# Window attention on one core: the square of a copied score tile as a 16-bit step of VectorE, 288 tiles off ScalarE, and a new order

## The chip, the cores and the metric

The kernel runs on one core of a Trainium2 chip. The metric is the device time of one execution in microseconds (us). The core has five engines that run side by side, each through its own instruction list in order, and that wait for each other by semaphores: TensorE (PE, matrix products into PSUM), ScalarE (ACT, here the exponential), VectorE (DVE), GpSimd (POOL, which works from SBUF to SBUF) and SyncE (SP, which issues DMAs).

## The reference

An image x of 224 x 224 pixels with 96 channels is projected to q, k and v. The first 48 channels attend within horizontal stripes 8 rows high, the last 48 within vertical stripes 8 columns wide, and the two halves are put side by side and projected once more.

```python
qkv = jnp.einsum('bhwc,cd->bhwd', x, wqkv)
q, k, v = qkv[..., :C], qkv[..., C:2 * C], qkv[..., 2 * C:]
scale = C2 ** (-0.5)                                   # C = 96, C2 = 48, sw = 8
qh = q[..., :C2].reshape(B * nh, sw * W, C2)           # 28 stripes of 1792 tokens
ah = _softmax(jnp.einsum('bqc,bkc->bqk', qh, kh) * scale, axis=-1)
oh = jnp.einsum('bqk,bkc->bqc', ah, vh).reshape(B, H, W, C2)
...                                                    # ov: the same over vertical stripes, channels C2:
o = jnp.pad(oh, ((0, 0), (0, 0), (0, 0), (0, C2))) + jnp.pad(ov, ((0, 0), (0, 0), (0, 0), (C2, 0)))
return jnp.einsum('bhwc,cd->bhwd', o, wo)
```

There are 56 stripes. Each needs 1792 x 1792 scores, and an exponential of every score.

## The kernel before

The stripes are done in 28 pairs P, one stripe in each half of the partitions. The 1792 queries of a pair are cut into chunks c of 512, 512, 512 and 256, and its keys into 14 groups of 128. A *tile* is a chunk against one group of keys (two groups for the short chunk): 128 partitions by 1024 scores, in two banks of PSUM. There are 28 x 49 = 1372 tiles, and there are three ways from scores to weights.

- *On ScalarE.* TensorE forms the scores (L670), ScalarE takes the exponential of all 1024 columns into a buffer PT in SBUF (L888), and TensorE multiplies it with V (L696). There were 1090 such tiles.
- *Off ScalarE, uncopied.* The scores are formed in banks 6 and 7 (L683). The exponential is made by writing the bits of a 16-bit float: the low part of the fixed-point score is the fraction, whose polynomial is a square plus a constant. VectorE takes the low half of each 32-bit score out of PSUM into a buffer `qb` (L1189), and the banks are given back. GpSimd squares it into PT (L1105). TensorE forms the same scores a second time, and VectorE adds their high part to the square (L1199). There were 180.
- *Off ScalarE, copied.* VectorE copies the whole 32-bit scores to `qb` (L1188), and TensorE need not form them again. Four steps follow: a shift and scale of the low halves into PT (L1108), the square in place in PT (L1109), a scale back into the low halves of `qb` (L1110), and the last conversion of `qb` to the bits in PT (L1111). Before, all four were GpSimd's. There were 102.

There are sixteen PT buffers, six `qb` buffers and three `tmp` buffers. VectorE also takes K, Q and V from PSUM to SBUF (L440, L451, L488) and the products with V (L1164), and it normalises the projected output: for the horizontal stripes into `Ph_sb` (L537, L545), for the vertical ones with `Ph_sb` added. That last step is done either in single tiles on VectorE (L593), or as a product of up to five tiles on VectorE into `tmp` (L580) with the sum on GpSimd (L584).

The order of all of this is made when the program is built. `Sched` keeps a clock for each engine with assumed durations (L25 to L37); `step_pe`, `step_dve` and `step_pool` choose the next instruction by those clocks, and `settle` and `emit` write the lists and the waits. A row of the table `HOW` stands for each pair: how many tiles of each of its chunks go off ScalarE (first string), and the thresholds by which the planner chooses. `backlog` adds up GpSimd's work in its queue, and by it the planner decides at L1187 whether a tile is copied, and at L1174 whether GpSimd is to do an output sum. `mids` lists the steps that follow L1188 or L1189, and `next_mid` puts each on the queue of its engine when the one before it has been issued. So a change of an assumed duration or of `HOW` moves instructions on every engine, and the built order is then fixed.

```python
            elif what == "p1":
                tl = it["t"]
                tl["whole"] = backlog(t) < 2.0 * how()[11]
```

Of the kernel before, what the change touches and what calls it, by code (L numbers as in the profile page):

```python
# [10 lines left out]
ALU = mybir.AluOpType  # L11
# [17 lines left out]
W_PE, W_FIN = 0.021, 0.06  # L29
SEMD, SEMP, SELF, SEMX = 0.15, 0.12, 0.19, 0.05  # L30
D_P1, D_SQ, D_ADD = 1.14, 1.852, 0.0019
D_TS, D_TW = 1.125, 1.28
L_SQ, L_TS, L_TW, LATE_TS = 1.96, 1.145, 1.43, 0.13


# [5 lines left out]


HOW = [
    ("023", 11, "242426002612 394226102014 324227102012 327227100012"),
    ("464", 7, "336319113442 331319113442 331319113442 335319113444"),
    ("323", 12, "521219112723 539418120834 539418120834 434418120234"),
    ("354", 10, "399238123332 399238123343 569429010920 569429110923"),
    ("334", 2, "383429102532 383429102532 383425102532 383135102532"),
    ("334", 9, "383135102932 546317021634 562226102334 5a7326002334"),
    ("342", 7, "5a7326102314 5a7325002311 568429003732 568429003730"),  # L50
    ("446", 5, "568429003733 433316102523 566439000041 566439000021"),
    ("233", 1, "475325003244 475325023241 475325123243 479325121243"),
    ("444", 0, "479325101243 479225101224 479225101221 479225101222"),
    ("224", 0, "479225100222 2a2327102823 2a5327102823 2a5317002823"),
    ("424", 3, "245217002823 245217002843 245217022843 245217020843"),
    ("544", 8, "381329000711 381329000911 247236022532 4a8425113033"),
    ("243", 4, "511318021714 511318021714 511318001724 4a5438023343"),
    ("444", 1, "4a5428023343 4a5436023343 312316012422 312336012422"),
    ("224", 6, "332236012422 372436010422 5a1219103932 521239103932"),
    ("334", 9, "521239002931 521239002932 421239002942 421239002942"),  # L60
    ("443", 2, "369428110343 369428110342 366425110342 273436003342"),
    ("343", 6, "273436001331 273436001423 273436001423 273336001422"),
    ("224", 9, "379316100602 358338000810 222419002813 222419002512"),
    ("342", 5, "232419002542 279339002241 279319002241 522136000512"),
    ("444", 10, "522438000513 3a2329000422 3a7119100312 453417001532"),
    ("443", 8, "453417021530 449415012722 489415012022 542214103644"),
    ("334", 9, "542214103641 388426102621 388426100622 201438102334"),
    ("334", 12, "201418103334 201418123333 466216100841 318216113541"),
    ("323", 2, "318217112542 218218112542 541117111741 5a9436000032"),
    ("333", 4, "5a9138000032 5a9138002032 333319101722 335319100722"),  # L70
    ("453", 11, "335119100722 5a6316122020 5a6315121020 5a6325101020"),
]
OFF = [[int(d) for d in k] + [0] for k, _, _ in HOW]
TAIL = [t for _, t, _ in HOW]
# [89 lines left out]
def bass_standalone__window_attn_cswin__vision_kernel(  # L164
# [27 lines left out]
    with es:  # L192
# [443 lines left out]
        for P in range(NP):  # L636
            for c in range(NCH):
# [5 lines left out]
                for i, kts in enumerate(groups):  # L643
                    t = dict(P=P, c=c, kts=kts, q0=CH_Q0[c], qs=sz, kind="A" if i < na else "P")
# [63 lines left out]
        pool_q = []  # L708
# [168 lines left out]
        def pt_keys(slot):  # L877
            return [("PT", slot)]
# [220 lines left out]
        def mids(tl):  # L1099

            i = tl["qb"]
            q, y = qb[i][:], PT[tl["slot"]][:].bitcast(FP16)
            qk, yk = [("q", i), "pser"], pt_keys(tl["slot"])
            if not tl["whole"]:
                return [("pool", (D_SQ, L_SQ, 0.0), lambda e: e.tensor_tensor(y, q, q, ALU.mult), qk, yk)]  # L1105
            lo = q.bitcast(U16).rearrange("p (n t) -> p n t", t=2)[:, :, 0]
            bits = PT[tl["slot"]][:].bitcast(U16)
            return [("pool", (D_TS, L_TS, LATE_TS), lambda e: e.tensor_scalar(y, lo, 2.0 ** -16, QH, ALU.mult, ALU.add), qk, yk),  # L1108
                    ("pool", (D_SQ, L_SQ, 0.0), lambda e: e.tensor_tensor(y, y, y, ALU.mult), yk + ["pser"], yk),  # L1109
                    ("pool", (D_TW, L_TW, LATE_TS), lambda e: e.tensor_scalar(lo, y, 65536.0 * P2, 65536.0 * QC0, ALU.mult, ALU.add), yk + ["pser"], [("q", i)]),  # L1110
                    ("pool", (D_TS, L_TS, LATE_TS), lambda e: e.tensor_scalar(bits, q, 1.0, 128.0 * (127.0 - SOFF), ALU.mult, ALU.add), qk, yk)]  # L1111

# [25 lines left out]
        def step_dve():  # L1138
# [30 lines left out]
            elif what == "fill":  # L1169
# [4 lines left out]
                if two and it["stage"] == 0:  # L1174
                    it["stage"] = 1 if backlog(t) < 1.5 * how()[9] else 2
                elif two and it["stage"] == 1:
                    it["stage"] = len(f["chain"])
                else:
                    it["stage"] += 1
# [5 lines left out]
# [3 lines that stand above are left out]
                S.commit("dve", t, D_P1, D_P1 + SEMD, lambda e: e.tensor_copy(  # L1188
                    qb[tl["qb"]][:], ps[:, PB0 * 512:(PB0 + 2) * 512]) if tl["whole"] else e.tensor_scalar(  # L1189
                    qb[tl["qb"]][:], half(U16, 0), QS * 2.0 ** -16, QS * QH, ALU.mult, ALU.add),  # L1190
                    PBK, [("q", tl["qb"])], fresh=[("q", tl["qb"])],
                    tag=("p1", tl["P"], tl["c"], tl["kts"][0]))
                ring[PB0] = ring[PB0 + 1] = None
                tl["mid"] = mids(tl)
                next_mid(tl)
            elif what == "f":
                tl = it["t"]
                ptk = pt_keys(tl["slot"])
                S.commit("dve", t, D_P1, D_P1 + SEMD, lambda e: e.scalar_tensor_tensor(  # L1199
                    PT[tl["slot"]][:].bitcast(U16), half(BF16, 1), 128.0 * (127.0 - SOFF + QC0),  # L1200
                    PT[tl["slot"]][:].bitcast(FP16), ALU.add, ALU.add),
                    PBK + ptk, ptk, tag=("f", tl["P"], tl["c"], tl["kts"][0]))
                ring[PB0] = ring[PB0 + 1] = None
                pv_ready[(tl["P"], tl["c"])].append((tl, tl["slot"]))
            else:
                m = it["m"]
                S.commit("dve", t, m[1], m[1] + SEMD, m[2], m[3], m[4])
                next_mid(it["t"])
# [6 lines left out]

        def backlog(t):
            return max(0.0, S.free["pool"] - t) + sum(
                1.0 if it["what"] == "add" else it["m"][1][0] + sum(m[1][0] for m in it["t"]["mid"]) for it in pool_q)

        def step_pool():  # L1220
            t = S.free["pool"]
# [31 lines left out]
        while pv_open[0] < len(pv_chunks) or fin_q or dve_q or pool_q:  # L1253
            e = min(("pe", "dve", "pool"), key=lambda k: S.free[k])
# [93 lines left out]
```

## Time and profile before

| what | before |
|---|---|
| time, median of 3 runs | 1017.89 us (1017.62 to 1017.92) |
| profiled execution, its own time | 1017.86 us |
| its span, first to last instruction | 1016.0 us |
| busy: TensorE, VectorE, ScalarE, GpSimd | 994.1, 927.0, 1005.9, 931.8 us |
| exponential tiles on ScalarE | 1090 |
| tiles off ScalarE: uncopied, copied | 180, 102 |

A row of the profile names a line of the kernel, an engine and an operation, then the tensor written, the tensors read, their shapes and types and the count; behind the bar stand the group's busy time in us and the mean of one in ns, and then the engine's idle time just before them with what ended it. A row of a timeline begins with the start and the length in us. The chain that ended last is followed back from the last instruction, at each step to what released it. On GpSimd the records of one instruction are rough, and neighbours on one engine can overlap in the records, so a busy time is not quite the sum of the means.

### The profile page before, as it was taken

The numbers are of one execution on the slowest core, as the hardware profiler recorded it, in microseconds if no ns is written. First come the engines' busy times: TensorE is split into PE (matmuls) and PEld (weight loads), VectorE is DVE, ScalarE is ACT, GpSimd is POOL, SyncE is SP. The second block draws the span as 40 slices with busy tenths as digits, with TensorE's granted clock in tenths as the row PEclk, the third lists the DMA queues.
The fourth block names the chain that finished last, engine by engine and source line by source line (L and its number), as shares of the span: only waits on it lengthen the run. The fifth ranks groups of instructions, "written<-read, shape, count | busy, mean of one in ns | idle before, by whom it ended". The sixth has DMA issues, their size and how long they took to land.

```text
span 1016.0 us, 31766 instructions
## 1 busy us (share of the span) xinstructions
PE 994.1 (98%) x13833; PEld 401.2 (39%) x13833; DVE 927.0 (91%) x1509; ACT 1005.9 (99%) x1101; POOL 931.8 (92%) x666
## 2 busy tenths in 40 slices
PE   9999999999999999999999999999999999999998
PEld 4434433433343344334334334333443433343343
DVE  7999899889998989899999999889999999999897
ACT  8999999999999999999999999999999999999997
POOL 5999999899999999998999999999889899999993
PEclk9999999999999999999999999999999999999999
DMA  4403203204202311220111221223313033313111
GB/s 87 98 28 65 67 14 65 66 2 79 65 2 65 79 34 34 65 38 13 28 38 23 56 54 25 51 57 65 53 20 62 18 59 55 61 21 57 24 21 37
DMA packets 162877, 47.08 MB, mean 46 GB/s; under 512 B 155895, under 2 KB 162711, under 8 KB 162738
## 3 DMA queue, kind: packets, MB, share of 16 engines
q1 hardware_dynamic: 161762, 44.59, 21.8%
q8 instruction: 108, 1.77, 0.7%
q10 hardware_dynamic: 976, 0.47, 0.2%
q14 instruction: 31, 0.25, 0.1%
HBM read 10.60 MB, written 19.28 MB: 29 GB/s over the span
## 4 chain that ended last, share of the span: by engine, by line
ACT 97%; PE 2%; DVE 0%; issue 0%; DVEq 0%
ACT PT L888 97%; PE ps L696 1%; PE ps L670 1%; PE ps L346 0%; ACT xT_sb L747 0%; PE ps L481 0%; PE ps L731 0%; DVE out_all L593 0%; PE ps L566 0%; PE ps L463 0%; DVE OT_sb L1164 0%; PE ps L435 0%; DVE warm L309 0%; DVE rc L573 0%; DVEq L192 0%
## 5 line engine op out<-in xcount | busy, mean ns | idle before, releaser
L888 ACT ACTIVATE PT<-ps 128x1024 bf16<-128x1024 f32 x1090 | 1001.5, 1078 | 1.3 <-PE ps L670 1.1
L670 PE MATMUL ps<-QT_sb,KT_sb 49*64 49x512 bf16 (+1 forms) x5144 | 446.0, 363 | 15.4 <-ACT PT L888 3.4
L696 PE MATMUL ps<-PT,V_sb 128*49 128x512 bf16 (+1 forms) x3136 | 451.5, 360 | 0.3 <-ACT PT L888 0.2
L1105 POOL TENSOR_TENSOR PT<-qb 128x1024 f16<-128x1024 f32 x180 | 337.8, 1893 | 8.8 <-DVE qb L1189 5.2
L670 PEld LDWEIGHTS ps<-QT_sb,KT_sb 49*64 49x64 bf16 x5144 | 129.3, 103 | 341.6 <-ACT PT L888 315.0
L1189 DVE TENSOR_SCALAR qb<-ps 128x1024 f32<-128x1024 uint16 x180 | 219.9, 1222 | 22.4 <-PE ps L683 20.1
L1199 DVE SCALAR_TENSOR_TENSOR PT<-ps,PT 128x1024 uint16<-128x1024 bf16 x180 | 219.7, 1221 | 17.3 <-PE ps L683 15.9
L696 PEld LDWEIGHTS ps<-PT,V_sb 128*49 128x49 bf16 x3136 | 134.7, 103 | 165.8 <-issue 130.2
L1109 POOL TENSOR_TENSOR PT<-PT 128x1024 f16<-128x1024 f16 x102 | 193.0, 1892 | 5.9
L683 PE MATMUL ps<-QT_sb,KT_sb 50*64 50x512 bf16 x1848 | 181.3, 382 | 1.3 <-DVE V_sb L488 0.2
L1110 POOL TENSOR_SCALAR qb<-PT 128x1024 uint16<-128x1024 f16 x102 | 137.4, 1347 | 8.8
L1108 POOL TENSOR_SCALAR PT<-qb 128x1024 f16<-128x1024 uint16 x102 | 106.5, 1044 | 33.0 <-DVE qb L1188 24.2
L1188 DVE COPY qb<-ps 128x1024 f32<-128x1024 f32 x102 | 124.6, 1221 | 7.9 <-PE ps L683 5.9
L1111 POOL TENSOR_SCALAR PT<-qb 128x1024 uint16<-128x1024 f32 x102 | 106.5, 1044 | 8.3
L451 DVE CAST QT_sb<-ps 128x512 bf16<-128x512 f32 (+1 forms) x111 | 67.6, 615 | 10.2 <-PE ps L435 9.9
L1164 DVE CAST OT_sb<-ps 113x512 bf16<-113x512 f32 x112 | 69.3, 618 | 5.7 <-PE ps L696 4.7
L440 DVE TENSOR_SCALAR_CACHE_REDUCE KT_sb<-ps 128x512 bf16<-128x512 f32 x108 | 65.9, 615 | 1.2 <-PE ps L435 0.6
L683 PEld LDWEIGHTS ps<-QT_sb,KT_sb 50*64 50x64 bf16 x1848 | 52.5, 104 | 33.3 <-DVE PT L1199 6.3
L545 DVE TENSOR_TENSOR Ph_sb<-ps,rc 128x480 bf16<-128x480 f32 (+1 forms) x84 | 52.4, 623 | 2.8
L488 DVE CAST V_sb<-ps 128x480 bf16<-128x480 f32 (+1 forms) x84 | 51.4, 619 | 3.3 <-PE ps L481 2.8
L584 POOL TENSOR_TENSOR out_all<-tmp,Ph_sb 128x480 bf16<-128x480 f32 (+1 forms) x48 | 49.8, 1046 | 3.2 <-DVE tmp L580 2.6
L593 DVE SCALAR_TENSOR_TENSOR out_all<-ps,rc,Ph_sb 128x96 bf16<-128x96 f32 x165 | 40.5, 310 | 1.1
(63 smaller groups left out, 416.2 us busy)
## 6 DMA issues: line engine op xcount, KB each, us to landing
cols_dram<-in_x_dram SPq DMA_DIRECT2D x28, 336.0 KB
out_dram<-out_all SPq DMA_DIRECT2D x387, 24.0 KB, 1.9
xT_sb<-cols_dram SPq DMA_TRANSPOSE x28, 4.6
xT_sb<-in_x_dram SPq DMA_TRANSPOSE x26, 4.6
xT_sb<-ones_dram SPq DMA_DIRECT2D x26, 7.0 KB
Ph_sb<-in_x_dram SPq DMA_DIRECT2D x2, 168.0 KB, 3.7
Ph_sb<-in_x_dram ACTq DMA_DIRECT2D x2, 168.0 KB, 3.9
out_dram<-out_all ACTq DMA_DIRECT2D x5, 24.0 KB, 1.9
```

What stands on the lines that cost most here:

```text
L670: ins = e.matmul(bank(SETS[s] + w)[64 * kh:64 * kh + 64, i * t["qs"]:(i + 1) * t["qs"]], lhsT=KT_sb[b][64 * w:64 * w + CA, kt * 128 + 64 * ...
L683: ins = e.matmul(bank(PB0 + w)[64 * kh:64 * kh + 64, 0:512], lhsT=KT_sb[b][64 * w:64 * w + nr, kt * 128 + 64 * kh:kt * 128 + 64 * kh + 64] ...
L696: ins = e.matmul(bank(pb)[64 * w:64 * w + CA, 0:t["qs"]], lhsT=V_sb[b][:, w, kt, :], rhs=PT[slot][:, ca:ca + t["qs"]], start=st and i == 0 ...
L888: S.commit("act", 0.0, D_ACT, None, lambda e, s=s, slot=slot: e.activation(PT[slot][:], ps[:, 512 * SETS[s]:512 * SETS[s] + 1024], ACTF.Ex ...
L1105: return [("pool", (D_SQ, L_SQ, 0.0), lambda e: e.tensor_tensor(y, q, q, ALU.mult), qk, yk)]
L1108: return [("pool", (D_TS, L_TS, LATE_TS), lambda e: e.tensor_scalar(y, lo, 2.0 ** -16, QH, ALU.mult, ALU.add), qk, yk), ("pool", (D_SQ, L_ ...
L1109: ("pool", (D_SQ, L_SQ, 0.0), lambda e: e.tensor_tensor(y, y, y, ALU.mult), yk + ["pser"], yk),
L1110: ("pool", (D_TW, L_TW, LATE_TS), lambda e: e.tensor_scalar(lo, y, 65536.0 * P2, 65536.0 * QC0, ALU.mult, ALU.add), yk + ["pser"], [("q", ...
L1111: ("pool", (D_TS, L_TS, LATE_TS), lambda e: e.tensor_scalar(bits, q, 1.0, 128.0 * (127.0 - SOFF), ALU.mult, ALU.add), qk, yk)]
L1188: S.commit("dve", t, D_P1, D_P1 + SEMD, lambda e: e.tensor_copy(qb[tl["qb"]][:], ps[:, PB0 * 512:(PB0 + 2) * 512]) if tl["whole"] else e.t ...
L1189: qb[tl["qb"]][:], ps[:, PB0 * 512:(PB0 + 2) * 512]) if tl["whole"] else e.tensor_scalar(
L1199: S.commit("dve", t, D_P1, D_P1 + SEMD, lambda e: e.scalar_tensor_tensor(PT[tl["slot"]][:].bitcast(U16), half(BF16, 1), 128.0 * (127.0 - S ...
```

## The change

The square L1109 of a copied tile goes from GpSimd to VectorE. It is the same product of PT with itself, 128 x 1024 in 16-bit floats, in place. The planner gets an assumed duration for it (`D_S2`), and `backlog` counts only those remaining steps that are GpSimd's. `HOW` is another table: 288 tiles go off ScalarE instead of 282. With it the built order differs on every engine: 212 tiles are copied and 76 are not, 1084 are on ScalarE, and of the output groups of the vertical stripes 30 instead of 48 are summed on GpSimd, and the others are VectorE's single tiles (254 instead of 165 instructions of L593).

```diff
 D_P1, D_SQ, D_ADD = 1.14, 1.852, 0.0019
-D_TS, D_TW = 1.125, 1.28
+D_TS, D_TW, D_S2 = 1.125, 1.28, 0.62
...
 HOW = [
-    ("023", 11, "242426002612 394226102014 324227102012 327227100012"),
-    ("464", 7, "336319113442 331319113442 331319113442 335319113444"),
...
+    ("022", 9, "466415000124 461417000104 465417003114 465417001114"),
+    ("555", 3, "465439001114 465439001114 468439001114 453229003612"),
...
             return [("pool", (D_TS, L_TS, LATE_TS), lambda e: e.tensor_scalar(y, lo, 2.0 ** -16, QH, ALU.mult, ALU.add), qk, yk),
-                    ("pool", (D_SQ, L_SQ, 0.0), lambda e: e.tensor_tensor(y, y, y, ALU.mult), yk + ["pser"], yk),
+                    ("dve", D_S2, lambda e: e.tensor_tensor(y, y, y, ALU.mult), yk, yk),
...
         def backlog(t):
             return max(0.0, S.free["pool"] - t) + sum(
-                1.0 if it["what"] == "add" else it["m"][1][0] + sum(m[1][0] for m in it["t"]["mid"]) for it in pool_q)
+                1.0 if it["what"] == "add" else it["m"][1][0] + sum(m[1][0] for m in it["t"]["mid"] if m[0] == "pool") for it in pool_q)
```

More of the change, by code (lines that the diff above doesn't have):

```diff
@@ L43 @@
 HOW = [
-    ("023", 11, "242426002612 394226102014 324227102012 327227100012"),
-    ("464", 7, "336319113442 331319113442 331319113442 335319113444"),
[L46 to L71, printed above, removed]
+    ("022", 9, "466415000124 461417000104 465417003114 465417001114"),
@@ new lines @@
+    ("555", 3, "465439001114 465439001114 468439001114 453229003612"),
+    ("222", 11, "411436001423 211436101423 565137111041 567137111041"),
+    ("454", 3, "586218001532 583218001532 588218011532 588318011534"),
+    ("334", 8, "387218000314 354228000643 557417000803 538116103321"),
+    ("434", 3, "578116103323 234214122542 234218122512 234228122512"),
+    ("324", 4, "565216102933 565218102933 565218102933 565228002933"),
+    ("545", 3, "304439103403 304439103403 224337001044 224137001044"),
@@ new lines @@
+    ("323", 3, "224237001644 388329102842 388329100822 388329100824"),
+    ("324", 10, "398429100821 398429100824 398419100824 398419100820"),
+    ("454", 11, "567238103444 567238102434 207338101144 317429002133"),
+    ("334", 11, "464327000504 354439101430 339439101434 339439101444"),
+    ("444", 8, "349439101444 349439101444 349419101444 349419001444"),
+    ("234", 11, "349119001444 349119000444 349419100544 394139002044"),
+    ("444", 11, "394119002044 494119002044 494219002044 494217002044"),
@@ new lines @@
+    ("333", 6, "494217000044 494237003044 494337003044 484336003044"),
+    ("325", 10, "484236003044 361217001820 561219001824 568219001224"),
+    ("334", 7, "579436000442 279436100442 479336100442 479336100442"),
+    ("344", 10, "279336102442 499316112321 499316113324 499316113344"),
+    ("444", 5, "499216103344 499216103344 243418102610 223418102612"),
+    ("223", 11, "223418102622 203418102621 5a5429100641 258318001820"),
+    ("344", 7, "278118102423 278118102423 249339003642 219339003344"),
@@ L72 @@
+    ("333", 12, "219319001343 219319001343 219319001344 219319101344"),
+    ("335", 11, "472138003623 422339001141 462339001141 475428000042"),
+    ("233", 10, "475418010043 475418110743 384439002424 384429002424"),
+    ("446", 9, "389437100343 389437100343 5a9437102343 3a9236101544"),
+    ("332", 9, "3a9216101544 2a9216101544 2a9216101542 438328112222"),
+    ("445", 10, "438338112224 333338112924 554428100012 551426100012"),
 ]
```

## The prediction

> **What bounds the kernel now.** I read the core's span first, then the page's busy shares, its chain that ended last, and the waits of ScalarE.
>
> ```profile
> span 1016.0 us, 31766 instructions
> PE 994.1 (98%) x13833; PEld 401.2 (39%) x13833; DVE 927.0 (91%) x1509; ACT 1005.9 (99%) x1101; POOL 931.8 (92%) x666
> ACT 97%; PE 2%; DVE 0%; issue 0%; DVEq 0%
> L888 ACT ACTIVATE PT<-ps 128x1024 bf16<-128x1024 f32 x1090 | 1001.5, 1078 | 1.3 <-PE ps L670 1.1
> 9.20 5.61 ACT L888 ACTIVATE PT<-ps 128x1024 bf16<-128x1024 f32 x6 [1.10 <-PE ps L670]
> 999.80 11.13 ACT L888 ACTIVATE PT<-ps 128x1024 bf16<-128x1024 f32 x12
> ```
>
> ScalarE (ACT) is the bound. Its 1090 exponentials run from 9.20 us to 999.80 + 11.13 = 1010.93 us and wait 1.3 us in all, so one costs (1010.93 - 9.20) / 1090 = 0.919 us from start to start. The span is that stretch, 9.2 us ahead of it and 5.1 us of last outputs. The profiled execution took 1017.86 us, 1.86 us more than its span, and stands at the median of the runs (1017.89), so sums against it need no correction.
>
> The two helpers are close behind. A tile taken off ScalarE goes over VectorE (DVE) and GpSimd (POOL), and these rows carry its price now:
>
> ```profile
> L1105 POOL TENSOR_TENSOR PT<-qb 128x1024 f16<-128x1024 f32 x180 | 337.8, 1893 | 8.8 <-DVE qb L1189 5.2 <-DVE wq_sb L467 0.3 <-DVE rc L537 0.2
> L1108 POOL TENSOR_SCALAR PT<-qb 128x1024 f16<-128x1024 uint16 x102 | 106.5, 1044 | 33.0 <-DVE qb L1188 24.2 <-DVE rc L573 1.4 <-DVE rc L537 0.9
> L1109 POOL TENSOR_TENSOR PT<-PT 128x1024 f16<-128x1024 f16 x102 | 193.0, 1892 | 5.9
> L1110 POOL TENSOR_SCALAR qb<-PT 128x1024 uint16<-128x1024 f16 x102 | 137.4, 1347 | 8.8
> L1111 POOL TENSOR_SCALAR PT<-qb 128x1024 uint16<-128x1024 f32 x102 | 106.5, 1044 | 8.3
> L584 POOL TENSOR_TENSOR out_all<-tmp,Ph_sb 128x480 bf16<-128x480 f32 x35 | 38.2, 1096 | 2.6 <-DVE tmp L580 2.0
> L584 POOL TENSOR_TENSOR out_all<-tmp,Ph_sb 128x384 bf16<-128x384 f32 x13 | 11.7, 913 | 0.6 <-DVE tmp L580 0.6
> ```
>
> **The change, part by part.** *ScalarE.* Off-tiles rise from 282 to 288, exponentials fall to 1084: 6 x 0.919 = 5.5 us saved if nothing else comes to set the pace, 1017.86 - 5.5 = 1012.4 us.
>
> *GpSimd by instruction counts.* In the built streams uncopied tiles fall from 180 to 76, copied ones rise from 102 to 212, and the adds of L584 fall from 48 to 30 (18 long, 12 short). GpSimd's work is 76 x 1.893 = 143.9, 212 x (1.044 + 1.347 + 1.044) = 728.2, and 18 x 1.096 + 12 x 0.913 = 30.7, together 902.8 us. Between two of its single-input steps it leaves a gap:
>
> ```profile
> 17.95 1.04 POOL L1108 TENSOR_SCALAR PT<-qb 128x1024 f16<-128x1024 uint16 x1 [7.30 <-DVE qb L1188]
> 19.08 1.89 POOL L1109 TENSOR_TENSOR PT<-PT 128x1024 f16<-128x1024 f16 x1
> 24.76 1.35 POOL L1110 TENSOR_SCALAR qb<-PT 128x1024 uint16<-128x1024 f16 x1
> 26.19 1.05 POOL L1108 TENSOR_SCALAR PT<-qb 128x1024 f16<-128x1024 uint16 x1
> 1000.43 3.74 POOL L1105 TENSOR_TENSOR PT<-qb 128x1024 f16<-128x1024 f32 x2 [4.38 <-DVE qb L1189]
> ```
>
> 19.08 - 17.95 - 1.044 = 0.086 and 26.19 - 24.76 - 1.347 = 0.083 us. With 0.083 us for each of 636 such steps (52.8 us) GpSimd needs 955.6 us. Its tile work begins at 17.95 us and ends at 1004.17, 11.8 us ahead of the span's end. Kept, these make 18.0 + 955.6 + 11.8 = 985.4 us. The span that ScalarE allows is 1016.0 - 5.5 = 1010.5, so GpSimd has 25 us to spare: 25 / 212 = 0.12 us per copied tile.
>
> *VectorE by instruction counts.* It loses 104 each of L1189 and L1199, gains 110 copies (L1188) and 212 squares, and finishes 18 fewer output groups by L580 and so 89 more output tiles by L593.
>
> ```profile
> 504.72 1.22 DVE L1189 TENSOR_SCALAR qb<-ps 128x1024 f32<-128x1024 uint16 x1
> 505.86 0.55 DVE L488 CAST V_sb<-ps 128x384 bf16<-128x384 f32 x1
> 507.85 0.66 DVE L545 TENSOR_TENSOR Ph_sb<-ps,rc 128x480 bf16<-128x480 f32 x1
> 508.42 1.22 DVE L1199 SCALAR_TENSOR_TENSOR PT<-ps,PT 128x1024 uint16<-128x1024 bf16 x1
> 511.41 0.68 DVE L1164 CAST OT_sb<-ps 113x512 bf16<-113x512 f32 x1
> 512.04 1.22 DVE L1199 SCALAR_TENSOR_TENSOR PT<-ps,PT 128x1024 uint16<-128x1024 bf16 x1
> 1009.07 1.89 DVE L593 SCALAR_TENSOR_TENSOR out_all<-ps,rc,Ph_sb 128x96 bf16<-128x96 f32 x8
> L1188 DVE COPY qb<-ps 128x1024 f32<-128x1024 f32 x102 | 124.6, 1221 | 7.9 <-PE ps L683 5.9
> L1164 DVE CAST OT_sb<-ps 113x512 bf16<-113x512 f32 x84 | 57.5, 685 | 4.4 <-PE ps L696 4.0
> ```
>
> Neighbours on VectorE overlap in the records, so I use start to start: 505.86 - 504.72 = 1.14 us for 1024 elements, 508.42 - 507.85 = 0.57 for the 480-element product, 1.89 / 8 = 0.236 for L593. The square has no row. If its 16-bit elements go two a cycle it costs what 512 elements cost, 512.04 - 511.41 = 0.63 us; one a cycle, 1.14. I take 0.63. The sum: -208 x 1.14 + 110 x 1.14 + 212 x 0.63 - 18 x 0.57 + 89 x 0.236 = +33 us, so VectorE is busy 927 + 33 = 960 of 1010 us. Some 12 us of its idle time lies at the ends (stretch and its length, then busy time and count of PE, PEld, DVE, ACT, POOL):
>
> ```profile
> 0.00:20.00 20.00, 18.24 (x209) 9.09 (x209) 13.46 (x39) 15.16 (x23) 8.33 (x32) 1.00 0.39 87
> 1000.00:1016.00 16.00, 11.70 (x186) 5.74 (x182) 10.52 (x32) 10.93 (x12) 3.74 (x2) 1.00 0.20 38
> ```
>
> (20.00 - 13.46 + 16.00 - 10.52 = 12.0.) What is left to spare is 1010.5 - 960 - 12 = 38 us, 0.18 us per square.
>
> *TensorE.* 104 fewer second score passes and 6 fewer exponential tiles take some 416 matmuls from the streams (1848 to 1456 on L683, 3576 to 3552 in the 512-column form of L670): only relief. *Output DMAs.* 392 as before, one moved from SP's queue to ScalarE's at the end: nothing.
>
> *The new waits.* The square waits on VectorE's in-order queue for GpSimd's L1108, and L1110 waits on GpSimd's queue for the square. Behind a waiting square stand copies and casts out of PSUM; TensorE needs those banks for the next scores and projections. Six qb buffers let several copied tiles be in flight, so while both engines keep time the waits are covered by other tiles' steps; with that cover gone, each costs its full length on both engines.
>
> *What the trace can't price: the square beside GpSimd.* Every long VectorE row has one stream from PSUM and at most one from SBUF. The square is the first with two SBUF streams (y and y). GpSimd is shown undisturbed only beside the former:
>
> ```profile
> L1105 POOL TENSOR_TENSOR PT<-qb x180: 1887/1892/1906, 20.9 to 1002.3; 128x1024 f16<-128x1024 f32 x180
> L1108 POOL TENSOR_SCALAR PT<-qb x102: 1044/1044/1047, 18.0 to 978.9; 128x1024 f16<-128x1024 uint16 x102
> ```
>
> (minimum, median, maximum in ns.) A gain is excluded, since the median is the minimum already. From below: nothing, each runs as if alone. From above: they exclude each other and GpSimd loses 0.63 us per square. Between them, if exclusion holds only while data stream: the square streams 1024 x (1221 - 685) / 512 / 2 = 0.536 us; an L584 add has 1.096 - 480 x (1.096 - 0.913) / 96 = 0.18 us that doesn't grow with its size, which with the gap of 0.083 hides 0.26, and 0.27 us is lost. I take exclusion with only the gap used, 0.63 - 0.08 = 0.55 us. GpSimd is the reason: its two-input square takes 1.892 against 1.044 for one input, so there streams of SBUF data are what is short, and it is under way nine tenths of the time (902.8 of 1010), so hardly a square finds it idle. GpSimd's sum is then 18.0 + 955.6 + 212 x 0.55 + 11.8 + 1.9 = 1104 us. VectorE comes out alike: a square that meets a running step waits half of it, weighted by length (the sum of squared durations, 1152, over twice their sum, 903) 0.64 us, nine times in ten 0.57, and 960 + 12 + 212 x 0.57 + 1.9 = 1095. ScalarE is fed by both and follows: **1104 us**.
>
> The Trainium skill, "SBUF — State Buffer", section "Who interferes with whom", has a rule for this: a VectorE instruction with two SBUF inputs contends with a GpSimd instruction that reads SBUF, as an exclusive lock for the whole instruction, and whichever starts second fully blocks. No row here shows it, there being no such instruction before; by it the sum would be the 1104, and without it 1012.
>
> **The rivals.** *A. They don't disturb each other* (other side). Both SBUF streams of the square are served beside GpSimd. Then both engines keep their spare 25 and 38 us, the waits are covered, ScalarE sets the end: 1012.4 us. For it: every steady row above. Against: none of those is beside an instruction of this kind. It decides only while a square costs GpSimd under 0.12 us and VectorE under 0.18; at 0.12 to 0.15 us per square gain and loss cancel, about 1012 to 1019.
>
> *B. The square runs one element a cycle*, with no meeting at all: VectorE 960 + 212 x 0.51 + 12 + 1.9 = 1082 us. For it: every VectorE row of 1024 elements takes 1.22. Against: all of these have 32-bit data or PSUM. The Trainium skill, "VectorE: DVE Perf Modes", section "The perf-mode tier table", gives `tensor_tensor` two elements a cycle for 16-bit operands in SBUF, so by that page B falls; no row here has one.
>
> *C. Light meeting*, 0.27 us per square: GpSimd 18.0 + 955.6 + 57.2 + 11.8 + 1.9 = 1045 us.
>
> **How the numbers follow.** Of the band from 0 to 0.63 us per square, four fifths lie above the 0.12 where the gain is gone, and I give slower about that: exclusion at 1104 has 0.55, C 0.16, B 0.05, A 0.21, and the narrow band around break-even 0.03 (within 0.2%, 2 us, about the least that a measurement of this kernel can tell). Faster 0.21, same 0.03, slower 0.76. The forecast's own range is 1045 (C) to 1150, where VectorE waits 0.83 us per square instead of 0.57 because both engines, full and in fixed order, delay each other (960 + 12 + 212 x 0.83 + 1.9). As A holds a fifth, the range for 8 in 10 starts below it: 1010 to 1150.
>
> **What would show it.** Right: L1109 on VectorE well over 0.68 us in mean, with a wide spread; L1108 and L1111 no longer at 1044 as minimum, median and maximum, or gaps before them; ScalarE idle tens of us, released by TensorE; the chain no longer 97% ScalarE. Wrong: GpSimd's durations unchanged and L1109 at 0.6 to 0.7, with ScalarE still waiting about 1 us (A), or L1109 steady at 1.2 us (B).

## The result and the profile after

The changed kernel takes 1100.95 us (median of 4 runs, 1094.06 to 1104.38) against 1017.78 us for the kernel before, a ratio of 1.0808 with a 95% interval from 1.0785 to 1.0832. The profiled execution took 1104.38 us. Ratios, here and below, rest on the runs within 1.5% of their kernel's fastest, which of four runs leaves out one of e8 and two each of e5 and e11. The page of the changed kernel, in the lines that answer to those shown of before:

```profile
span 1102.6 us, 31129 instructions
PE 1012.1 (92%) x13421; PEld 394.3 (36%) x13421; DVE 1011.4 (92%) x1694; ACT 1021.9 (93%) x1095; POOL 964.4 (87%) x772
PEclk9997998999899999999999899999999999999998
DVE 40%; POOL 32%; PE 18%; ACT 7%; issue 2%; DVEq 0%
L888 ACT ACTIVATE PT<-ps 128x1024 bf16<-128x1024 f32 x1084 | 1017.5, 1045 | 71.4 <-PE ps L670 66.3
L1110 POOL TENSOR_SCALAR qb<-PT 128x1024 uint16<-128x1024 f16 x212 | 300.4, 1428 | 49.1 <-DVE PT L1109 37.4
L1108 POOL TENSOR_SCALAR PT<-qb 128x1024 f16<-128x1024 uint16 x212 | 248.0, 1170 | 49.2 <-DVE qb L1188 34.7
L1111 POOL TENSOR_SCALAR PT<-qb 128x1024 uint16<-128x1024 f32 x212 | 231.1, 1090 | 17.0
L1109 DVE TENSOR_TENSOR PT<-PT 128x1024 f16<-128x1024 f16 x212 | 219.5, 1037 | 16.0 <-POOL PT L1108 15.7
```

The chain that ended last was 97% ScalarE; now it winds through VectorE and GpSimd, 72% of it, with 7% left to ScalarE. ScalarE does six exponentials less and waits 71.4 us ahead of them instead of 1.3. No engine is over 93% busy, so no single engine is simply full. The instructions themselves have changed, though. The answers for single lines (minimum, median, maximum in ns; the last row is L1110 of before):

```profile
L1109 DVE TENSOR_TENSOR PT<-PT x212: 647/907/2398, 20.7 to 1089.4; 128x1024 f16<-128x1024 f16 x106
L1108 POOL TENSOR_SCALAR PT<-qb x212: 1047/1047/1555, 18.9 to 1086.9; 128x1024 f16<-128x1024 uint16 x106
L1110 POOL TENSOR_SCALAR qb<-PT x212: 1330/1347/1899, 22.4 to 1090.1; 128x1024 uint16<-128x1024 f16 x106
L1110 POOL TENSOR_SCALAR qb<-PT x102: 1337/1347/1362, 24.8 to 989.8; 128x1024 uint16<-128x1024 f16 x102
```

The square can be done in 0.647 us, but its mean is 1.037 and its longest 2.4 us. GpSimd's steps, which before lay within 25 ns of each other, now reach half a microsecond beyond their median. The timeline shows how the two meet. Rows of GpSimd first, then of VectorE:

```profile
506.09 1.05 POOL L1111 TENSOR_SCALAR PT<-qb 128x1024 uint16<-128x1024 f32 x1
507.75 1.34 POOL L1110 TENSOR_SCALAR qb<-PT 128x1024 uint16<-128x1024 f16 x1 [0.62 <-DVE PT L1109]
511.81 1.05 POOL L1108 TENSOR_SCALAR PT<-qb 128x1024 f16<-128x1024 uint16 x1 [0.45 <-DVE qb L1188]
513.48 1.34 POOL L1110 TENSOR_SCALAR qb<-PT 128x1024 uint16<-128x1024 f16 x1 [0.62 <-DVE PT L1109]
```

```profile
506.54 1.14 DVE L1109 TENSOR_TENSOR PT<-PT 128x1024 f16<-128x1024 f16 x1
512.24 1.15 DVE L1109 TENSOR_TENSOR PT<-PT 128x1024 f16<-128x1024 f16 x1
513.92 1.38 DVE L1109 TENSOR_TENSOR PT<-PT 128x1024 f16<-128x1024 f16 x1
```

Each square starts in the middle of a GpSimd step and ends about half a microsecond after that step's end: 507.68 against 507.14, 513.39 against 512.86, 515.30 against 514.82. Those 0.48 to 0.54 us are close to the 0.536 us that the prediction estimated for the square's stream. So it looks as if the square streams only when the step is done, whenever it was started.

### The profile page after: what moved, and what is told of

The parts are those of the page before. It is cut to its first block, busy times and chain, and to the rows that moved or that the text cites. A ratio compares the mean times of both kernels' runs of the same rounds, so it can differ in the third digit from the quotient of the medians.

```text
span 1102.6 us, 31129 instructions
## 1 busy us (share of the span) xinstructions
PE 1012.1 (92%) x13421; PEld 394.3 (36%) x13421; DVE 1011.4 (92%) x1694; ACT 1021.9 (93%) x1095; POOL 964.4 (87%) x772
## 4 chain that ended last, share of the span: by engine, by line
DVE 40%; POOL 32%; PE 18%; ACT 7%; issue 2%; DVEq 0%
DVE PT L1109 12%; DVE qb L1188 11%; POOL qb L1110 10%; POOL PT L1108 8%; POOL PT L1111 7%; PE ps L696 7%; ACT PT L888 7%; POOL PT L1105 6%; PE ps L670 6%; DVE PT L1199 3%; DVE out_all L593 3%; PE ps L683 2%; DVE OT_sb L1164 2%; DVE QT_sb L451 2%; DVE KT_sb L440 2%
## 5 line engine op out<-in xcount | busy, mean ns | idle before, releaser
L888 ACT ACTIVATE PT<-ps 128x1024 bf16<-128x1024 f32 x1084 | 1017.5, 1045 | 71.4 <-PE ps L670 66.3
L1110 POOL TENSOR_SCALAR qb<-PT 128x1024 uint16<-128x1024 f16 x212 | 300.4, 1428 | 49.1 <-DVE PT L1109 37.4
L1108 POOL TENSOR_SCALAR PT<-qb 128x1024 f16<-128x1024 uint16 x212 | 248.0, 1170 | 49.2 <-DVE qb L1188 34.7
L1188 DVE COPY qb<-ps 128x1024 f32<-128x1024 f32 x212 | 257.9, 1217 | 15.9 <-PE ps L683 15.0
L1111 POOL TENSOR_SCALAR PT<-qb 128x1024 uint16<-128x1024 f32 x212 | 231.1, 1090 | 17.0
L1109 DVE TENSOR_TENSOR PT<-PT 128x1024 f16<-128x1024 f16 x212 | 219.5, 1037 | 16.0 <-POOL PT L1108 15.7
L683 PE MATMUL ps<-QT_sb,KT_sb 50*64 50x512 bf16 x1456 | 149.3, 399 | 40.7 <-DVE qb L1188 16.6
L1105 POOL TENSOR_TENSOR PT<-qb 128x1024 f16<-128x1024 f32 x76 | 147.8, 1960 | 6.4 <-DVE qb L1189 3.1
L1199 DVE SCALAR_TENSOR_TENSOR PT<-ps,PT 128x1024 uint16<-128x1024 bf16 x76 | 92.6, 1219 | 11.3 <-POOL PT L1105 5.5
L1189 DVE TENSOR_SCALAR qb<-ps 128x1024 f32<-128x1024 uint16 x76 | 92.6, 1218 | 6.9 <-PE ps L683 6.4
L1164 DVE CAST OT_sb<-ps 113x512 bf16<-113x512 f32 x112 | 68.9, 615 | 9.5 <-PE ps L696 8.7
L593 DVE SCALAR_TENSOR_TENSOR out_all<-ps,rc,Ph_sb 128x96 bf16<-128x96 f32 x254 | 61.5, 309 | 0.8 <-DVE rc L573 0.2
L545 DVE TENSOR_TENSOR Ph_sb<-ps,rc 128x480 bf16<-128x480 f32 (+1 forms) x84 | 52.1, 621 | 1.8
L435 PE MATMUL ps<-xT_sb,w_sb 97*64 97x512 bf16 x224 | 41.1, 372 | 8.1 <-DVE qb L1188 2.5
```

The costliest lines, as they stand in the source:

```text
L593: return e.scalar_tensor_tensor(out_sb[b][:, w, kt, :], bk3[:, s, 0:C], rc[ri][:, s:s + 1], Ph_sb[:, kt, j, :], ALU.mult, ALU.add)
L683: ins = e.matmul(bank(PB0 + w)[64 * kh:64 * kh + 64, 0:512], lhsT=KT_sb[b][64 * w:64 * w + nr, kt * 128 + 64 * kh:kt * 128 + 64 * kh + 64] ...
L888: S.commit("act", 0.0, D_ACT, None, lambda e, s=s, slot=slot: e.activation(PT[slot][:], ps[:, 512 * SETS[s]:512 * SETS[s] + 1024], ACTF.Ex ...
L1109: ("dve", D_S2, lambda e: e.tensor_tensor(y, y, y, ALU.mult), yk, yk),
```

## The experiments

Three theories were to be told apart. *Exclusion*: the square, with two streams from SBUF, and a GpSimd step that reads SBUF keep each other out. *Length*: VectorE is full with 212 more instructions. *Handover*: the extra waits between the engines, or the new order, can't be kept.

**Single steps by themselves (e4).** A kernel of its own: 24 of each step on one engine, each waiting for the one before it, alone and then beside 24 of a step on the other engine. Its list of phases, the step on VectorE first (the rest of the kernel isn't shown):

```diff
+        PHASES = [
+            (square, None), (None, low), (None, writes), (None, two),
+            (square, low), (square, writes), (square, two),
+            (one_stream, None), (one_stream, low),
+            (from_psum, low), (psum_and_sbuf, low),
+            (copy16, None), (copy16, low), (half_square, low),
+        ]
```

> Not the kernel: single steps measured by themselves, 24 of each, alone and side by side on VectorE and GpSimd; nothing of the reference is computed. Exclusion theory: the square alone about 0.65 us, L1108's step alone 1.04 us; side by side the two take turns, so that 24 of each take about 24 x (0.54 + 1.04) = 38 us instead of 27, and a square or a step is stretched by up to the other's length; beside constant writes on GpSimd the square stays at 0.65 us; a VectorE step with one SBUF stream, a copy from PSUM, and a PSUM-and-SBUF sum leave GpSimd's step at 1.04 us. A 16-bit copy from SBUF to SBUF may disturb too. Length and handover theories: every pair at the lengths that each has alone.

Its timeline, start and length in us of the runs of 24 or 48; L34 is the square, L52 GpSimd's single-input step, L55 its constant write, L58 its own square, L43 VectorE's copy from PSUM, L46 its sum of a PSUM and an SBUF stream, L37 the half square:

```profile
3.16 17.40 DVE L34 TENSOR_TENSOR y<-y 128x1024 f16<-128x1024 f16 x24
20.65 27.04 POOL L52 TENSOR_SCALAR g<-q 128x1024 f16<-128x1024 uint16 x24 [18.08 <-DVE y L34]
119.40 33.85 DVE L34 TENSOR_TENSOR y<-y 128x1024 f16<-128x1024 f16 x24 [98.83 <-POOL g L58]
119.53 34.63 POOL L52 TENSOR_SCALAR g<-q 128x1024 f16<-128x1024 uint16 x24 [0.16 <-POOL g L58]
154.19 17.40 DVE L34 TENSOR_TENSOR y<-y 128x1024 f16<-128x1024 f16 x24 [0.94 <-POOL g L52]
154.28 24.17 POOL L55 MEMSET g<- 128x1024 f16 x24
251.18 27.04 POOL L52 TENSOR_SCALAR g<-q 128x1024 f16<-128x1024 uint16 x24 [17.39 <-DVE h L40]
278.37 27.04 POOL L52 TENSOR_SCALAR g<-q 128x1024 f16<-128x1024 uint16 x24 [0.15 <-POOL g L52]
308.50 27.04 POOL L52 TENSOR_SCALAR g<-q 128x1024 f16<-128x1024 uint16 x24 [3.09 <-DVE r L43]
378.40 28.07 POOL L52 TENSOR_SCALAR g<-q 128x1024 f16<-128x1024 uint16 x24 [0.36 <-DVE z L49]
378.43 28.32 DVE L37 TENSOR_TENSOR y<-y 128x512 f16<-128x512 f16 x24
```

Alone, a square takes 17.40 / 24 = 0.725 us from start to start and GpSimd's step 27.04 / 24 = 1.127. Side by side they keep step with each other at 34.63 / 24 = 1.443: GpSimd loses 0.316 us per square and VectorE 33.85 / 24 - 0.725 = 0.69. Beside GpSimd's constant writes the square is back at 17.40. Beside the one-stream sum of pairs (251.18), a copy from PSUM (278.37) and a sum with one stream from PSUM and one from SBUF (308.50) GpSimd takes its 27.04 again. Beside GpSimd's own two-input square (L58) the loss is alike: 24 of these take 55.20 us instead of 47.24 alone, 0.33 us more each. So the exclusion is there, between the square and GpSimd's reads from SBUF; the expected 38 us for the pair were 35, so a part of each step lies outside it. Which property of the square brings it about isn't separated. It has two SBUF streams, but also a higher rate: 1024 elements in 0.692 us, against 512 in 0.686 for the sum of pairs and 1024 in 1.224 for the two steps with PSUM. No run has two SBUF streams at the lower rate. The half square is the odd one: it costs GpSimd only 28.07 / 24 - 1.127 = 0.04 us, yet it waits as the whole one does (28.32 / 24 = 1.18 us each).

The rule of the Trainium skill, "SBUF — State Buffer", section "Who interferes with whom", is borne out for these pairs: the square with its two SBUF inputs collides with GpSimd's reads and not with its writes, and the three steps with at most one SBUF input leave GpSimd alone. Its size is not: an exclusive lock for the whole instruction would cost the step about what the square takes alone, 0.692 us, and 0.316 was measured.

**The same order without the second stream (e2).** Only the square's body differs from the changed kernel.

```diff
-                    ("dve", D_S2, lambda e: e.tensor_tensor(y, y, y, ALU.mult), yk, yk),
+                    ("dve", D_S2, lambda e: e.tensor_reduce(y[:, 0:256], y[:, 512:1024].rearrange("p (n t) -> p n t", t=2), mybir.AxisListType.X, ALU.add), yk, yk),
```

> The changed kernel with the square replaced by an instruction of about the same length with one SBUF stream instead of two: a sum of pairs over 512 of the 16-bit elements of the same PT buffer, 256 results. The square itself is left out of the computation. Same order and waits. Exclusion theory: 1012 to 1017 us, VectorE as busy per step as with an undisturbed square (about 0.65 us in the record), GpSimd's steps at their old lengths. Length theory: 1090 to 1105 us, since VectorE does as much as before. Handover theory: 1085 to 1105 us.

1012.35 us (1012.02 to 1012.86), a ratio of 0.9948 (0.9933 to 0.9963). Its page:

```profile
span 1010.7 us, 31129 instructions
PE 973.7 (96%) x13421; PEld 390.9 (39%) x13421; DVE 936.7 (93%) x1694; ACT 999.8 (99%) x1095; POOL 904.2 (89%) x772
L888 ACT ACTIVATE PT<-ps 128x1024 bf16<-128x1024 f32 x1084 | 995.3, 1093 | 1.5 <-PE ps L670 1.1
L1109 DVE TENSOR_REDUCE PT<-PT 128x256 f16<-128x512 f16 x212 | 142.4, 674 | 0.6 <-POOL PT L1108 0.6
```

With the same order, the same waits and an instruction of 0.674 us in the square's place, everything fits: ScalarE waits 1.5 us. Length and handover fall. The stand-in also reads less from SBUF, 512 elements in one stream instead of 1024 in each of two, so this run alone doesn't say what about the square collides. This kernel is also the measure for the changed one: its GpSimd is busy 904.2 us against 964.4 (0.28 us more per square), its VectorE 936.7 against 1011.4 (0.35 more), its span 91.9 us shorter.

**A square of 8 columns (e1).**

```diff
-e.tensor_tensor(y, y, y, ALU.mult)
+e.tensor_tensor(y[:, 0:8], y[:, 0:8], y[:, 0:8], ALU.mult)
```

> The changed kernel with the square L1109 shortened to 8 of its 1024 columns; the other 1016 columns stay unsquared, so that part of the computation is left out. Order, waits, table and every other instruction are those of the changed kernel. Exclusion theory (the square and a GpSimd step that reads SBUF keep each other out while they stream): nothing is left to exclude, ScalarE is the bound again, 1012.4 us (1011 to 1015), L1108 back at 1047 ns throughout, ScalarE waiting under 5 us. Handover theory (the two extra handovers per copied tile, or the new order, can't be kept whatever the square costs): 1085 to 1105 us. Length theory (VectorE is simply full with 212 more squares, GpSimd plays no part): also 1012, so this run doesn't tell it from exclusion.

1017.71 us, ratio 1.0006 (0.9997 to 1.0016): 5 us more than expected, and more than e2, which has more to do. The rows of its squares and of L1108:

```profile
L1109 DVE TENSOR_TENSOR PT<-PT 128x8 f16<-128x8 f16 x212 | 111.7, 528 | 0.8 <-POOL PT L1108 0.6
L1109 DVE TENSOR_TENSOR PT<-PT x212: 115/440/1877, 20.1 to 1001.8; 128x8 f16<-128x8 f16 x106
L1108 POOL TENSOR_SCALAR PT<-qb x212: 1047/1047/1095, 18.3 to 999.3; 128x1024 f16<-128x1024 uint16 x106
```

An instruction of 0.115 us takes 0.528 in the mean and up to 1.877, nearly a whole L1105. That is VectorE's wait for its turn, 0.41 us, measured by itself, while GpSimd loses next to nothing (busy 905.7 us against 904.2 in e2). That waits as uneven as these cost more than an even 0.674 us is the likely reason for the 5 us, but no run separates it.

**GpSimd writes instead of reading (e3).** The full square, and on GpSimd constant writes in place of the three steps.

```diff
-lambda e: e.tensor_scalar(y, lo, 2.0 ** -16, QH, ALU.mult, ALU.add)
+lambda e: e.memset(y, 1.0)
-lambda e: e.tensor_scalar(lo, y, 65536.0 * P2, 65536.0 * QC0, ALU.mult, ALU.add)
+lambda e: e.memset(q, 1.0)
-lambda e: e.tensor_scalar(bits, q, 1.0, 128.0 * (127.0 - SOFF), ALU.mult, ALU.add)
+lambda e: e.memset(y, 1.0)
```

> The changed kernel with the full square on VectorE, and GpSimd's three steps of a copied tile (L1108, L1110, L1111) replaced by constant writes of 1024 elements to the same buffers, which read nothing from SBUF; that part of the computation is left out. Same order and waits; 76 squares L1105 and 30 adds still read. Exclusion theory, if only reads collide: 1011 to 1025 us, L1109 near 0.65 us in median. Exclusion theory, if writes collide too: 1060 to 1105 us. Length and handover theories: 1085 to 1105 us, as far as the writes are as long as the steps (about 1.0 us against 1.04 to 1.35).

1019.26 us, ratio 1.0027 (1.0008 to 1.0046), within what exclusion of reads alone expected. The square's row, which now meets only L1105 and the adds:

```profile
L1109 DVE TENSOR_TENSOR PT<-PT x212: 648/681/2265, 20.4 to 1003.2; 128x1024 f16<-128x1024 f16 x106
```

A constant write is shorter than the step it replaces, 0.952 us against 1.05 to 1.35, and GpSimd is busy only 765.5 us here. So the time alone doesn't single out the reads. The square's median does, 0.681 us instead of 0.907, together with the writes of e4.

**Which side sets the time (e8, e9, e10, e7).** Exclusion costs both engines. e8 puts back VectorE's wait alone, e9 GpSimd's loss alone, e10 both, all without a whole square; e7 halves it. The cuts show the lines put in; `pad` is a buffer that nothing else uses, and the lines that make it and count `k` are left out.

```diff
 e8, VectorE:
+lambda e: (e.tensor_tensor(y[:, 0:8], y[:, 0:8], y[:, 0:8], ALU.mult), e.tensor_reduce(y[:, 256:512], y[:, 512:1024].rearrange("p (n t) -> p n t", t=2), mybir.AxisListType.X, ALU.add))[1]
 e9, VectorE the sum of pairs alone, and GpSimd's L1110:
+lambda e: (e.memset(pad[:, 192 * k:192 * k + 192], 0.0), e.tensor_scalar(lo, y, 65536.0 * P2, 65536.0 * QC0, ALU.mult, ALU.add))[1]
 e10: both
 e7:
+e.tensor_tensor(y[:, 0:512], y[:, 0:512], y[:, 0:512], ALU.mult)
```

> VectorE's side of the exclusion alone: in place of the square a square of 8 columns, which has to wait for its turn but holds GpSimd up for next to nothing, and behind it the sum of pairs with one SBUF stream, of a square's length. The square itself is left out of the computation. VectorE then spends about 0.53 + 0.6 = 1.1 us on it, as on the contended square (1.04 us), and GpSimd loses nothing. If VectorE's wait sets the pace: 1085 to 1110 us. If GpSimd's loss does: 1012 to 1025 us. If it takes both: 1030 to 1070 us.

> GpSimd's side of the exclusion alone: on VectorE the undisturbed sum of pairs with one SBUF stream in place of the square (which is left out of the computation), and on GpSimd one constant write of 192 elements more ahead of each L1110, about 0.29 us, which is what GpSimd's records gained per square (60 us over 212). If GpSimd's loss sets the pace: 1070 to 1105 us. If VectorE's wait does: 1012 to 1025 us. If it takes both: 1030 to 1070 us.

> Both sides of the exclusion put back by hand, with no whole square in it: VectorE's wait for its turn (a square of 8 columns, then the one-stream sum of pairs) and GpSimd's loss (a constant write of 192 elements ahead of each L1110). The square itself is left out of the computation. If VectorE's wait and GpSimd's loss are the whole of what the square costs: 1090 to 1115 us, near the changed kernel. If the changed kernel has a third loss: under 1085 us. By the two runs before, the sides cost 77 and 36 us one by one, so they don't simply add if the time comes near 1101.

> The changed kernel with the square over 512 of the 1024 columns (the other half stays unsquared and is left out of the computation). In the measurement of single steps a half square lengthened GpSimd's step by only 0.04 us, against 0.32 for a whole one, while it still waited for its turn. If GpSimd's lost time sets the pace: 1012 to 1022 us. If VectorE's wait for its turn sets it: the wait stays (about 0.4 us) but the instruction is 0.27 us shorter, so 1040 to 1070 us.

| kernel, all in the changed kernel's order | ratio to before | us beyond e2 |
|---|---|---|
| e2, neither side | 0.9948 (0.9933 to 0.9963) | 0 |
| e9, GpSimd's loss alone | 1.0310 (1.0280 to 1.0339) | 36 |
| e8, VectorE's wait alone | 1.0669 (1.0607 to 1.0731) | 75 |
| e10, both | 1.0707 (1.0689 to 1.0725) | 78 |
| the changed kernel | 1.0808 (1.0785 to 1.0832) | 89 |
| e7, half squares | 1.0227 (1.0212 to 1.0243) | 28 |

(The last column is the difference of the medians from 1012.35, over the runs that the ratios rest on. For e8 that median is 1087.69; over all four of its runs it is 1089.59, which gives the 77 in the expectation of e10.) The rows of the stand-ins, of e8 first and then of e9:

```profile
L888 ACT ACTIVATE PT<-ps 128x1024 bf16<-128x1024 f32 x1084 | 1014.5, 1049 | 48.1 <-PE ps L670 43.0
L1110 POOL TENSOR_SCALAR qb<-PT 128x1024 uint16<-128x1024 f16 x212 | 283.3, 1343 | 80.7 <-DVE PT L1109 68.9 <-DVE wq_sb L467 2.8 <-DVE rc L573 1.3
L1109 DVE TENSOR_REDUCE PT<-PT 128x256 f16<-128x512 f16 x212 | 142.9, 674 | 0.0
L1109 DVE TENSOR_TENSOR PT<-PT 128x8 f16<-128x8 f16 x212 | 110.4, 521 | 1.5 <-POOL PT L1108 1.4
```

```profile
L888 ACT ACTIVATE PT<-ps 128x1024 bf16<-128x1024 f32 x1084 | 1008.4, 1060 | 24.3 <-PE ps L670 20.3
L1110 POOL MEMSET pad<- 128x192 bf16 x212 | 54.7, 258 | 12.9 <-DVE PT L1109 5.5
L1109 DVE TENSOR_REDUCE PT<-PT 128x256 f16<-128x512 f16 x212 | 143.7, 679 | 38.6 <-POOL PT L1108 38.0
```

VectorE's wait for its turn is the larger side. Its stand-in is somewhat too long (0.521 + 0.674 = 1.195 us against 1.037), so the 75 us are an upper figure. The two sides don't add: once VectorE is late, GpSimd has idle time to lose (e8's L1110 waits 68.9 us for the square's stand-in). Together they come to 78 of 89 us (1090.37 us, at the foot of the 1090 to 1115 that were expected), so no large third loss is to be seen. A small one isn't excluded, since the stand-ins aren't exact: VectorE is busy 1018.8 us in e10 against 1011.4 in the changed kernel, GpSimd 955.9 against 964.4. e7 came out at the foot of the range for VectorE's wait (1040.75 us, for 1040 to 1070). The half square takes 0.819 us, and its shortest record is 0.380, so less than half of it is work; GpSimd is busy only 0.07 us more per square than in e2 (919.1 against 904.2 us).

```profile
L1109 DVE TENSOR_TENSOR PT<-PT 128x512 f16<-128x512 f16 x212 | 173.3, 819 | 6.1 <-POOL PT L1108 5.6
```

**The old table (e5, e11).** The square on VectorE with the table of before, and then the same with the one-stream sum.

```diff
 e5: the changed kernel with
-    ("022", 9, "466415000124 461417000104 465417003114 465417001114"),
+    ("023", 11, "242426002612 394226102014 324227102012 327227100012"),
...
 e11: e5 with
-e.tensor_tensor(y, y, y, ALU.mult)
+e.tensor_reduce(y[:, 256:512], y[:, 512:1024].rearrange("p (n t) -> p n t", t=2), mybir.AxisListType.X, ALU.add)
```

> One part of the change alone: the square on VectorE, with the table HOW of before. 282 tiles go off ScalarE as before; the planner copies 187 of them and leaves 95 uncopied, in an order of its own. Exclusion theory: slower without the new table too. GpSimd needs 95 x 1.893 + 187 x 3.435 + about 60 for 58 sums + 561 x 0.083 = 929 us instead of 956, so a little more is covered: 1045 to 1090 us. If the new table were at fault: 1016 to 1025 us, as before.

> The kernel with the old table and the square on VectorE, but the square replaced by the one-stream sum of pairs (the square is left out of the computation); same order as with the old table. If the exclusion is all that made that kernel slower than the changed one: 1017 to 1022 us, since ScalarE has 1090 tiles. If the order that the planner makes from the old table has idle time of its own, because the table's thresholds were chosen for squares on GpSimd: 1030 to 1050 us.

e5 has a ratio of 1.1109 (1.1083 to 1.1136; 1128.19 and 1132.72 us), slower than the changed kernel and beyond what any theory expected. e11 says why: without the second stream that order still has 1.0407 (1.0323 to 1.0492), while the new table's has 0.9948. So the old table, with squares on VectorE, gives an order that is 4% worse in itself, and the exclusion adds 0.070 to the ratio, close to the 0.086 that it adds in the new order. Both ratios rest on two runs each, and a part of both may go with TensorE's clock, 0.949 in e5's profiled execution and 0.984 in e11's (see the last section). The new table is not the fault; it is what makes the order without exclusion good.

No run points to a version that beats both kernels: the only faster one, e2, leaves the square out.

## Why the prediction was right

The time, its sign and the mechanism came out as forecast, 1104 against 1100.95 us. That the time came so near is luck in part: two terms were too large, and a third that belongs in the sum was missing.

- *ScalarE.* Six exponentials at 0.919 us, 1012.4 us if nothing else comes: e2 gave 1012.35. Right.
- *GpSimd by counts*, 902.8 us of tile work and 25 us to spare: e2 is busy 904.2 us and keeps up. Right. *VectorE by counts*, 960 us: 936.7 with the stand-in, so the count was some 23 us too high and VectorE had more to spare than the 38 us; more than that was used up.
- *The square*, 0.63 us at two elements a cycle: its shortest record is 0.647, and 0.692 alone in e4. Right, and rival B with it falls.
- *GpSimd's loss*, taken as 0.55 us per square: 0.316 side by side, 0.28 in the kernel. Too large by three quarters. The lower bound of 0.27, from what of a step doesn't stream, was the right size. The step "exclusion with only the gap used" failed: of the 0.63 us it let only the gap of 0.08 cost nothing, and side by side 0.63 - 0.316 = 0.31 us cost nothing.
- *VectorE's wait*, taken as 0.57 us: 0.41 in e1, 1.037 - 0.647 = 0.39 in the changed kernel. Too large by four tenths or more. The forecast let squares come at random moments of a step and kept them waiting to its end; which of the two was wrong, no run separates. This side, which the forecast put a little below GpSimd's (1095 against 1104), is the larger one in the stand-ins (75 us against 36).
- *"ScalarE is fed by both and follows"*: the step that failed in the other direction. With the measured sizes the two sums give 18.0 + 955.6 + 212 x 0.316 + 11.8 + 1.9 = 1054 us for GpSimd and, with the 936.7 us of e2, 936.7 + 12 + 212 x 0.39 + 1.9 = 1033 us for VectorE, but the kernel took 1101. Each sum lets its engine run without further gaps. In the changed kernel GpSimd is idle 1102.6 - 964.4 = 138 us, where its sum has 83 for the ends and the gaps, and VectorE 91, where its sum has 12. In part each waits for the other in a fixed order (37.4 us for the square, 34.7 for `qb`, 15.7 for L1108); in part both wait for a TensorE whose clock has dropped (last section). The prediction had put such waits only into the upper end of its range, and the clock nowhere. So the 1104 was nearer than its terms deserve: about 50 us of oversized terms stood in for about 47 us of idle time that was not in it.
- *Rival A* falls: a square costs GpSimd 0.28 us and VectorE 0.35, over the 0.12 and 0.18 from which it would have failed. *Rival C* had GpSimd's loss right and the time, 1045, wrong, for the same missing term; e9, that loss alone, came to 1049.
- *The signs.* L1109 spread widely, L1108 and L1111 no longer stand at their minimum throughout (means of 1170 and 1090 ns), ScalarE waits 71.4 us, 66.3 of them on TensorE, and the chain is no longer ScalarE's: all four as named.

## What to carry to other kernels

An engine pair's independence is shown only for the kinds of operand that the trace shows side by side; here every VectorE row beside GpSimd had one SBUF stream at most, and the first with two brought both into lockstep. Price such a step as its own length and the wait for the running step of the other engine on top: 8 columns waited as long as 1024. And where three engines stand within a few per cent of the bound in a fixed order, the price per step divided by the spare time decides the sign, but the idle time that follows has to be in the sum as well, and with it what a pause does to TensorE's clock.

## What was not expected of the hardware

The half square costs GpSimd 0.04 us and the whole one 0.316: of streams of 0.27 and 0.536 us (the prediction's estimate) that leaves 0.22 us both times which cost GpSimd nothing. Where in its step that time lies, no run shows. A 16-bit copy from SBUF to SBUF, with one input, is held up as well, so a second input isn't needed for it: alone it takes 0.427 us, beside GpSimd's step 1.150, and it costs GpSimd little (rows of the windows 338 to 349.9 us and 349.9 to 378 us of e4):

```profile
L49 DVE COPY z<-y 128x1024 f16<-128x1024 f16 x24 | 10.2, 427 | 0.9
L49 DVE COPY z<-y 128x1024 f16<-128x1024 f16 x24 | 27.6, 1150 | 0.9
L52 POOL TENSOR_SCALAR g<-q 128x1024 f16<-128x1024 uint16 x24 | 26.2, 1092 | 16.3 <-DVE z L49 14.4
```

TensorE's granted clock, 1.000 before, fell to 0.972 in the profiled execution. The trace shows how. In most stretches of 20 us it is 1.00, in a few it is far lower (a stretch and its length, then busy time and count of PE, PEld, DVE, ACT and POOL, the clock, the DMA share and GB/s):

```profile
80.00:100.00 20.00, 19.93 (x242) 8.40 (x238) 14.21 (x21) 14.58 (x16) 12.28 (x11) 0.62 0.01 2
100.00:120.00 20.00, 19.60 (x260) 7.49 (x258) 18.65 (x33) 19.92 (x23) 17.38 (x15) 1.00 0.35 82
```

In finer windows the clock is 0.50 from about 78 to 95 us, and just ahead of that TensorE stood still for 1.67 us, until VectorE's L545 was done. There are eight such stretches at about half the clock (counted in windows of 2 us), of 4 to 18 us, some 70 us in all. Seven of them begin within a microsecond of the end of a pause of TensorE of 1.0 to 1.7 us, the eighth after several shorter pauses. So the pause comes first and the clock follows. In these stretches TensorE is busy nearly all the time (17.02 of the first 17.20 us) and the others wait for it: ScalarE is idle 27 of the 70 us, against 43 of the 1010 us around them. At the rate outside, 70 us would have 3, so some 24 of ScalarE's 71.4 us of waiting go with the halved clock. The exclusion makes VectorE late, TensorE pauses for it, and TensorE is slow for a while afterwards.

The four runs agree in size: 1094.06 us at 0.986, 1099.82 at 0.981, 1102.09 at 0.978, 1104.38 at 0.972. Continued at that rate (10.3 us for 0.014) to 1.000, some 20 of the 89 us would go with the clock. At 0.986, the clock of the fastest of these four, two runs of e10 took 1090.70 and 1091.65 us, so little is left between the two kernels. The mean clock alone doesn't fix the time, though: one run of e1 took 1021.96 us at 0.946, only 4 us above that kernel's median, and there is no trace of that run.
